# One converted weight block fewer ahead of the experts, four raw buffers, and product results in the ring of row tiles

## The chip, the cores and the metric

The kernel runs on one core of a Trainium2 chip, as a single program. Times are device microseconds (us) of one execution. Before the change three runs took 1015.66 us in the median (1014.09 to 1018.92).

## The reference

```python
# 1. a linear recurrence over time, for 4 batches x 8 heads, 768 steps, D = 48
a = a_re + i a_im, shortened to modulus <= 0.999
S_t = a_t * S_{t-1} + k_t v_t^T          # complex state, D x D
y_t = q_t @ Re(S_t)
x = y as 3072 rows of 384
# 2. one of 8 experts for each row, F = 1024
e = argmax(x @ w_gate);  p = softmax(x @ w_gate)[e]
x = p * (relu(x @ w1[e]) @ w2[e])
# 3. a gated layer; w1, w2, w3, w_out are doubles
out = ((x @ v1) * (x @ v2)) @ w3 @ w_out
```

The last two factors are one: the kernel makes `wf = w3 @ w_out` (1024 x 384) and multiplies by that.

## The kernel before, in words

The program has three stages on one time line. Up to about 407 us it works out the recurrence, in three groups of time steps with eight units each; the rows that come out (`xo`, tiles of 128 x 384 in a ring of six, `XB`) are routed in pairs: transposes `rt` (L122), logits `rl` (L131) copied to `lg` (L132), a chain on VectorE (`mx` L137, `key` L140, `kx` L142, `oh` L144), the rank of each row within its expert by a matmul `rk` (L148, L150), `r`, `pos`, `pi` on VectorE (L152 to L156), and an indirect DMA `xs<-xo,pi` on POOL that scatters the rows in DRAM by expert (L160). From about 444 us the experts run: `xe<-xs` (L385) reads one expert's rows, `px` (L395) transposes them, and 64 steps follow of nine matmuls into `ph` and nine into `py` each (L350 to L352, three for each product, since a weight or a value is a high and a low half). From about 700 us the last layer runs, with `wf` read back as `m2o`.

Beside that the kernel prepares `wf`. The class `Fuse` does it in two streams. The first converts doubles to a pair of fp32r halves in 24 conversion units: 8 factors `wo` of `w_out` (128 x 384), then 16 halves (128 x 512) of the 8 blocks of `w3`. Each unit has a raw buffer `fdr` of 512 KB, loaded from SyncE (SP) by `doubles` (L291), and three steps, of which the loop in `halves` runs the first for unit n beside the second for unit n-1 and the third for unit n-2: first VectorE's L336, L337, L339, then ScalarE's L329 and L330, then VectorE's L322, L323, L324. The raw buffer is free after L324. `ahead` issues the loads three units early. The second stream, `product`, makes the product blocks: 24 matmuls (L350 to L352) into `Wf`, or `wpo` within the experts, a ScalarE copy `ws` (L722), and a store `wf<-ws` by SP (L723). There is one buffer `ws`.

The constant `BEFORE` sets both how many blocks are converted by the end of the recurrence's third group, where `groups` (L1110 to L1145) runs one or two conversion units after each step of the recurrence's chain, and how many product blocks `build` issues ahead of the experts. `W3B` is the number of converted blocks kept at a time: `product` may run the next conversion units as long as `ready < min(f + W3B, BEFORE)`. The rest of the blocks, with their conversion units, are made within the experts, one piece for each step (`next(product, None)`). When the product stream has ended, its pools are left, and `moe2_weights` starts as the next stream in the experts: it loads `v1` and `v2` as `fdr<-in_v` from POOL (L291), converts them by `from_double` (L304 to L310), and reads `m2o<-wf` (L516), which `split` (L345, L346) turns into halves.

The order of each engine's instructions is set by the framework's scheduler, which simulates a time line and gives earlier-issued work the priority; `issue_after` moves a piece to the priority of another instruction. Pools and rings set the waits: a tile that takes a buffer waits until the last reader of its previous tile is done.

Of the kernel before, what the change touches and what calls it, by code (L numbers as in the profile page):

```python
# [8 lines left out]
F32 = mybir.dt.float32  # L9
F32R = mybir.dt.float32r  # L10
I32 = mybir.dt.int32
U32 = mybir.dt.uint32
U16 = mybir.dt.uint16
# [7 lines left out]
DM = 384  # L21
# [3 lines left out]
NF = 8  # L25
# [252 lines left out]
def ahead(load, srcs, n):  # L278

    got = []  # L280
    for i in range(len(srcs)):
        while len(got) < min(i + n, len(srcs)):
            got.append(load(srcs[len(got)]))
        yield got[i]


def doubles(pool, dma, bufs=RAW):

    def load(src):
        raw = pool.tile([128, 512, 2], I32, tag="fdr", name="fdr", bufs=bufs)[:, : src.shape[-1]]  # L290
        dma.dma_start(raw.rearrange("p n c -> p (n c)"), src.bitcast(I32))  # L291
        return raw

    return load
# [18 lines left out]
def halves(S, nc, raws, rest, units):  # L313

    v, act = nc.vector, nc.scalar
    first, second = [], []
    for n in range(len(units) + 2):
        if second:
            place, raw, m = second.pop()
            H, L = place()  # L320
            hi, lo = raw[:, :, 1].bitcast(F32), raw[:, :, 0].bitcast(F32)
            v.tensor_tensor(out=H, in0=hi, in1=m.bitcast(F32), op=ALU.mult)  # L322
            v.tensor_scalar(out=m, in0=H.bitcast(I32), scalar1=-0x800000, scalar2=None, op0=ALU.bitwise_and)  # L323
            v.scalar_tensor_tensor(out=L, in0=lo, scalar=2.0 ** -20, in1=m.bitcast(F32), op0=ALU.mult, op1=ALU.mult)  # L324
        if first:
            second.append(first.pop())
            _, raw, m = second[0]
            hi = raw[:, :, 1].bitcast(F32)
            act.activation(out=m, in_=m, func=AF.Relu, scale=8.0, bias=S.rebias)  # L329
            act.activation(out=hi, in_=hi, func=AF.Sign)  # L330
        if n < len(units):
            raw = next(raws)
            k = raw.shape[1]
            m = rest.tile([128, 512], I32, tag="fdm", name="fdm", bufs=2)[:, :k]
            low = rest.tile([128, 512], U16, tag="fdl", name="fdl")[:, :k]
            v.tensor_scalar(out=m, in0=raw[:, :, 1], scalar1=0x7FFFFE00, scalar2=None, op0=ALU.bitwise_and)  # L336
            v.tensor_scalar(out=low, in0=raw.bitcast(U16)[:, :, 2], scalar1=0x1FF, scalar2=None, op0=ALU.bitwise_and)  # L337
            lo = raw[:, :, 0]
            v.scalar_tensor_tensor(out=lo.bitcast(F32), in0=lo.bitcast(U32), scalar=2.0 ** -32, in1=low, op0=ALU.mult, op1=ALU.add)  # L339
            first.append((units[n], raw, m))  # L340
        yield
# [7 lines left out]
def mm3(nc, out, lh, ll, rh, rl, first, last):  # L349
    nc.tensor.matmul(out, lh, rh, start=first, stop=False)  # L350
    nc.tensor.matmul(out, lh, rl, start=False, stop=False)  # L351
    return nc.tensor.matmul(out, ll, rh, start=False, stop=last)  # L352
# [317 lines left out]
class Fuse:  # L670
# [10 lines left out]
    def _singles(self):  # L681
        nc, S, wp = self.nc, self.S, self.wp
        self.wo = [wp.tile([128, NF, DM], F32R, tag=f"wo{x}", name=f"wo{x}") for x in "hl"]
        self.w3 = []

        def factor(f):
            return lambda: [x[:, f] for x in self.wo]

        def block(f, h):
            def place():  # L690
                if not h:
                    pool = wp if f % W3B == 0 else self.w2p
                    self.w3.append([pool.tile([128, NF, 128], F32R, tag=f"w3{x}{f % W3B}", name=f"w3{x}{f}") for x in "hl"])
                return [x.rearrange("p g c -> p (g c)")[:, h * 512 : (h + 1) * 512] for x in self.w3[f]]
            return place

        srcs = [S.w_out[f * 128 : (f + 1) * 128, :] for f in range(NF)]
        srcs += [S.w3[f, :, h * 512 : (h + 1) * 512] for f in range(NF) for h in range(2)]
        raws = ahead(doubles(self.w2p, nc.sync, 5), srcs, 3)
        made = halves(S, nc, raws, wp, [factor(f) for f in range(NF)] + [block(f, h) for f in range(NF) for h in range(2)])  # L700
        for n in range(len(srcs) + 2):
            with self.tc.issue_after(S.end.ins):
                next(made)
            self.ready = max((n - 1 - NF) // 2, 0)
            yield

    def product(self):
        nc = self.nc
        for f in range(NF):
            while self.ready <= f:  # L710
                next(self.units)
                yield 0
            wh, wl = self.w3[f]
            po = self.psum(f, f"wpo_{f}")
            for g in range(NF):
                mm3(nc, po[:, :DM], wh[:, g], wl[:, g], self.wo[0][:, g], self.wo[1][:, g], g == 0, g == NF - 1)
                if g % 2 and g < NF - 1:
                    if self.ready < min(f + W3B, BEFORE):
                        next(self.units)
                    yield 960  # L720
            ws = self.w2p.tile([128, DM], F32, tag="ws", name=f"ws_{f}")
            nc.scalar.copy(ws, po[:, :DM])  # L722
            nc.sync.dma_start(self.S.wf[f * 128 : (f + 1) * 128, :], ws)  # L723
            self.blocks = f + 1
            yield 960
# [38 lines left out]
class Attn:  # L764
# [329 lines left out]
    def groups(self, route, side, free):  # L1094

        nc, S, st = self.nc, self.S, self.st
        self.ca, self.cb, self.cc, self.at, self.qkT, self.xs = {}, {}, {}, {}, {}, []
        self.route = route
        self.nv = self.slot = 0
        self.held = {}  # L1100
        self.pool, self.turns = [], 0
        self.spare = None
        self.vz = st.tile([128, VBUF, 2, HD], F32, tag="vz", name="vz")
        nc.gpsimd.memset(self.vz, 0.0)
        for q in range(2):
            self.ca[q] = st.tile([R2, 2, HD], F32, tag=f"ca{q}", name=f"ca{q}")
            self.cc[q] = st.tile([R2, 2, HD], F32, tag=f"cc{q}", name=f"cc{q}")
            nc.gpsimd.memset(self.ca[q], 0.0)
        yield lambda: self.made >= NPC
        self.W = self.pp.tile([128, 2, 512], F32, tag="W", name="W")  # L1110
        work = [(g, q, c) for g in range(NG) for q in range(2) for c in range(4)]
        ld = {}
        step = 0
        for n, u in enumerate(work):
            g, q, c = u
            if q == 0 and c == 0:
                while self.pool and self.made < (g + 1) * NPC:
                    yield self.fill(1)
                yield lambda: self.made >= (g + 1) * NPC
                yield from self.ends(g)  # L1120
                for x in work[n : n + 2]:
                    ld[x] = self.loads(x)
                if g == NG - 1:
                    yield free
                    singles = side.fuse.units
                    side()
            self.pool.append(Item("scores", self.scores(u, ld[u][1])))
            for x in self.chain(u, ld.pop(u)):
                yield x
                yield self.fill(S.fillcost)  # L1130
                step += 1
                if g == NG - 1:
                    for _ in range(1 + (step % 3 == 0)):
                        if side.fuse.ready < min(BEFORE, side.fuse.blocks + W3B):
                            next(singles, None)
            for x in work[n + 1 : n + 3]:
                if x[0] == g and x not in ld:
                    ld[x] = self.loads(x)
        self.spare = ()
        while self.pool:  # L1140
            yield self.fill(1)
# [138 lines left out]
FILL = 2600  # L1280
XB = 6
ZROWS = {i: [i] for i in range(NE)}
BEFORE = 6
W3B = 4


def build(ctx, tc, S):
# [8 lines left out]
    with ExitStack() as at:  # L1296
# [21 lines left out]
        def first():  # L1318
            z = x.ep.tile([128, 3 * DM // 8], F32, tag="zr", name="zr")
            nc.gpsimd.memset(z, 0.0)  # L1320
            yield from x.elementwise(lambda i: zero_rows(tc, S, z, ZROWS.get(i, [])), factors)
            for p in (e2, qp):
                p.__exit__(None, None, None)
            side.pools.append(tc.tile_pool(name="wf2", bufs=1, side="right"))
            side.fuse.w2p = side.pools[1].__enter__()
            done.append(1)
# [4 lines left out]
        drive([first(), second()])  # L1331
        while side.fuse.blocks < BEFORE:
            with tc.issue_after(x.lasty.ins):
# [62 lines left out]
```

## Time and profile before

| | us |
|---|---|
| median of three runs | 1015.66 (1014.09 to 1018.92) |
| the profiled execution | 1012.96 |
| its span, first to last instruction | 1011.2 |
| first matmul of the product (`Wf`) | 406.79 |
| first transpose of the experts (`px`) | 443.82 |
| first load `fdr<-in_v` issued | 501.23 |

The mean granted TensorE clock is 0.948 of full speed. The profile's first part gives the busy time and its share of the span for each engine: TensorE (PE) is busy for 896.7 us (89%), VectorE (DVE) for 610.1 us (60%), ScalarE (ACT) for 488.8 us (48%) and POOL for 126.8 us (13%). These are averages over three stages, so the rows further down are read by stretch. In all views a time is a start in us from the start of the span, and what stands in brackets is how long the engine stood idle before an instruction and what released it.

### The profile page before, as it was taken

Reading aid. Unit: us, or ns where it says so; the run is one execution under the profiler, and the core shown is the slowest. Engines: PE = TensorE matmul, PEld = TensorE weight load, DVE = VectorE, ACT = ScalarE, POOL = GpSimd, SP = SyncE. Lnnn points to the kernel's source line nnn. Section 1 sums busy time; section 2 is a strip of 40 time slices with the busy share of each in tenths; the row PEclk is TensorE's granted clock in tenths of the full one; section 3 lists DMA queues with packets and bytes.
Section 4 is the critical chain, followed back from the end, with each engine's and each line's share of the span. In section 5 each row is a group of like instructions: output and inputs, shape, how many; then the busy total and the mean of one; then the engine's idle time right before and its main releaser. Section 6 shows DMA issues by size and latency. Waiting matters only on the chain. (4 is left out here: it accounts for less than half of the span.)

```text
span 1011.2 us, 17058 instructions
## 1 busy us (share of the span) xinstructions
PE 896.7 (89%) x6402; PEld 762.8 (75%) x6402; DVE 610.1 (60%) x1374; ACT 488.8 (48%) x1089; POOL 126.8 (13%) x197
## 2 busy tenths in 40 slices
PE   3544899968897899969989999998999999999997
PEld 1222478655786787969978999997888888888886
DVE  6899899797996797545379996443232323232222
ACT  6455588764874786424355665453222222121211
POOL 5111000102010101000222221110001010101011
PEclk9666899989998999979999999999999999999999
DMA  5556985339544973544585765550000000000000
GB/s 188 178 177 197 293 264 180 127 110 346 167 162 132 345 241 104 164 124 131 127 267 163 190 155 131 141 92 2 1 1 32 1 32 1 32 1 32 2 30 31
DMA packets 90183, 128.74 MB, mean 127 GB/s; under 512 B 7233, under 2 KB 72689, under 8 KB 90097
## 3 DMA queue, kind: packets, MB, share of 16 engines
q1 hardware_dynamic: 76300, 82.61, 29.0%
q0 software_dynamic: 10688, 40.36, 11.3%
q10 hardware_dynamic: 3108, 4.65, 1.8%
q8 instruction: 51, 0.84, 0.3%
q14 instruction: 36, 0.29, 0.1%
HBM read 92.38 MB, written 35.22 MB: 126 GB/s over the span
## 5 line engine op out<-in xcount | busy, mean ns | idle before, releaser
L605 DVE TENSOR_TENSOR ab<-asb,pb 128x512 f32<-128x512 f32 x48 | 33.0, 688 | 188.2 <-PE pb L352 184.9
L346 DVE TENSOR_TENSOR l<-w,h 128x384 fp32r<-128x384 f32 x128 | 70.8, 556 | 70.4 <-ACT h L345 64.3
L345 ACT CAST h<-w 128x384 fp32r<-128x384 f32 x128 | 65.4, 514 | 98.2 <-PE ph L351 50.5
L600 ACT COPY asb<-pa 128x512 f32<-128x512 f32 x48 | 28.2, 586 | 121.1 <-PE pa L352 117.2
L804 PE MATMUL x<-s,ident 128*128 128x384 f32 x64 | 35.6, 692 | 48.6 <-ACT s L856 48.4
L345 ACT CAST gh<-ab 128x512 fp32r<-128x512 f32 x48 | 29.8, 620 | 95.2 <-DVE ab L605 90.7
L351 PE MATMUL py<-hl,h 128*128 128x432 f32 x192 | 70.4, 367 | 2.9 <-DVE hl L407 2.8
L350 PE MATMUL py<-hh,h 128*128 128x432 f32 x192 | 69.7, 363 | 2.8 <-ACT hh L406 2.8
L350 PE MATMUL ph<-xh,h 128*128 128x432 f32 x192 | 69.9, 366 | 0.2 <-DVE hl L407 0.2
L352 PE MATMUL ph<-xh,l 128*128 128x432 f32 x192 | 69.6, 363 | 0.0
L351 PE MATMUL ph<-xl,h 128*128 128x432 f32 x192 | 69.4, 361 | 0.0
L352 PE MATMUL py<-hh,l 128*128 128x432 f32 x192 | 69.3, 361 | 0.0
L848 DVE TENSOR_TENSOR pr<-cf,P 128x192 f32<-128x192 f32 x189 | 66.7, 354 | 3.1
L351 PE MATMUL po<-ol,gh 128*128 128x384 f32 x192 | 64.9, 338 | 0.0
L350 PE MATMUL po<-oh,gh 128*128 128x384 f32 x192 | 64.8, 337 | 0.0
L352 PE MATMUL po<-oh,gl 128*128 128x384 f32 x192 | 64.0, 338 | 0.0
L961 PE MATMUL tr<-ident,kk 128*96 128x128 f32 x384 | 57.1, 281 | 6.9 <-DMA kk<-qkd 3.9
L804 PEld LDWEIGHTS x<-s,ident 128*128 128x128 f32 x64 | 15.0, 257 | 63.6 <-ACT s L856 54.6
L569 POOL DMA_INDIRECT out<-ob,mdp x24 | 23.8, 993 | 305.9 <-DVE ob L568 164.2
L962 ACT COPY qkT<-tr 96x512 f32<-96x512 f32 x96 | 53.3, 589 | 16.2 <-PE tr L961 12.9
L350 PE MATMUL pa<-yh,ah 128*128 128x512 f32 x144 | 57.0, 396 | 3.0 <-ACT yh L345 3.0
L351 PE MATMUL pb<-yl,bh 128*128 128x512 f32 x144 | 57.0, 396 | 0.0
(219 smaller groups left out, 2388.2 us busy)
## 6 DMA issues: line engine op xcount, KB each, us to landing
w<-in_w SPq DMA_DIRECT2D x128, 192.0 KB
kk<-qkd SPq DMA_DIRECT2D x24, 768.0 KB
qkd<-qk POOLq DMA_DIRECT2D x21, 768.0 KB
qkr<-in_qk SPq DMA_DIRECT2D x24, 384.0 KB
a<-in_a SPq DMA_DIRECT2D x11, 768.0 KB
fdr<-in_w SPq DMA_DIRECT2D x16, 512.0 KB
fdr<-in_v POOLq DMA_DIRECT2D x12, 512.0 KB
xs<-zr POOLq DMA_DIRECT2D x8, 648.0 KB
```

The source lines that it names most:

```text
L345: nc.scalar.copy(H, src)
L346: nc.vector.tensor_tensor(out=L, in0=src, in1=H.bitcast(F32), op=ALU.subtract)
L350: nc.tensor.matmul(out, lh, rh, start=first, stop=False)
L351: nc.tensor.matmul(out, lh, rl, start=False, stop=False)
L352: return nc.tensor.matmul(out, ll, rh, start=False, stop=last)
L569: nc.gpsimd.indirect_dma_start(out=S.outv[j], out_offset=bass.IndirectOffsetOnAxis(ap=S.mdp[:, j, 0:1], axis=0), in_=ob, in_offset=None, b ...
L600: nc.scalar.copy(asb, pa)
L605: nc.vector.tensor_tensor(out=ab, in0=asb, in1=pb, op=ALU.mult)
L804: nc.tensor.matmul(p, S.ident, s[r], start=r == 0, stop=r == 1)
L848: v.tensor_tensor(out=pr, in0=twice(cf[i][:, t]), in1=bc(pv, 2, 1), op=ALU.mult)
L961: nc.tensor.transpose(pt[:, h], qk[:, h0 + h, w], self.S.ident)
L962: nc.scalar.copy(qkT[:, w, h0 : h0 + 4], pt)
```

## The change

`BEFORE` goes from 6 to 5 and `W3B` from 4 to 5. So 18 units are converted for the blocks ahead of the experts instead of 20, all five blocks fit into buffers of their own, and the third of the last three product blocks joins the two that the experts already held. The chain's steps issue one and two units in turn instead of two at each third step. There are four raw buffers (the default `RAW`) instead of five and loads are issued two units early instead of three. The converted blocks 0 and 1 of each five lie in the first pool, and the masks `fdm` in two single buffers of two pools instead of two buffers of one. `ws` takes a buffer of the ring `xo` of six.

```diff
--- before.py
+++ after.py
@@ -331,8 +331,8 @@
         if n < len(units):
             raw = next(raws)
             k = raw.shape[1]
-            m = rest.tile([128, 512], I32, tag="fdm", name="fdm", bufs=2)[:, :k]
-            low = rest.tile([128, 512], U16, tag="fdl", name="fdl")[:, :k]
+            m = rest[n % 2].tile([128, 512], I32, tag="fdm", name="fdm")[:, :k]
+            low = rest[0].tile([128, 512], U16, tag="fdl", name="fdl")[:, :k]
             v.tensor_scalar(out=m, in0=raw[:, :, 1], scalar1=0x7FFFFE00, scalar2=None, op0=ALU.bitwise_and)
             v.tensor_scalar(out=low, in0=raw.bitcast(U16)[:, :, 2], scalar1=0x1FF, scalar2=None, op0=ALU.bitwise_and)
             lo = raw[:, :, 0]
@@ -689,15 +689,15 @@
         def block(f, h):
             def place():
                 if not h:
-                    pool = wp if f % W3B == 0 else self.w2p
+                    pool = wp if f % W3B < 2 else self.w2p
                     self.w3.append([pool.tile([128, NF, 128], F32R, tag=f"w3{x}{f % W3B}", name=f"w3{x}{f}") for x in "hl"])
                 return [x.rearrange("p g c -> p (g c)")[:, h * 512 : (h + 1) * 512] for x in self.w3[f]]
             return place
 
         srcs = [S.w_out[f * 128 : (f + 1) * 128, :] for f in range(NF)]
         srcs += [S.w3[f, :, h * 512 : (h + 1) * 512] for f in range(NF) for h in range(2)]
-        raws = ahead(doubles(self.w2p, nc.sync, 5), srcs, 3)
-        made = halves(S, nc, raws, wp, [factor(f) for f in range(NF)] + [block(f, h) for f in range(NF) for h in range(2)])
+        raws = ahead(doubles(self.w2p, nc.sync), srcs, 2)
+        made = halves(S, nc, raws, (wp, self.w2p), [factor(f) for f in range(NF)] + [block(f, h) for f in range(NF) for h in range(2)])
         for n in range(len(srcs) + 2):
             with self.tc.issue_after(S.end.ins):
                 next(made)
@@ -718,7 +718,7 @@
                     if self.ready < min(f + W3B, BEFORE):
                         next(self.units)
                     yield 960
-            ws = self.w2p.tile([128, DM], F32, tag="ws", name=f"ws_{f}")
+            ws = self.S.rpool.tile([128, DM], F32, tag="xo", name=f"ws_{f}", bufs=self.S.xbufs)
             nc.scalar.copy(ws, po[:, :DM])
             nc.sync.dma_start(self.S.wf[f * 128 : (f + 1) * 128, :], ws)
             self.blocks = f + 1
@@ -1130,7 +1130,7 @@
                 yield self.fill(S.fillcost)
                 step += 1
                 if g == NG - 1:
-                    for _ in range(1 + (step % 3 == 0)):
+                    for _ in range(1 + step % 2):
                         if side.fuse.ready < min(BEFORE, side.fuse.blocks + W3B):
                             next(singles, None)
             for x in work[n + 1 : n + 3]:
@@ -1280,8 +1280,8 @@
 FILL = 2600
 XB = 6
 ZROWS = {i: [i] for i in range(NE)}
-BEFORE = 6
-W3B = 4
+BEFORE = 5
+W3B = 5
 
 
 def build(ctx, tc, S):
```

The scheduler then gives each engine another order. The first place is VectorE at the end of the recurrence, its last 12 instructions before the last step of the chain and the routing that follows it. `at` (L993) masks the scores, `cb` and `W` (L1061, L1062) are the chain's last step, and L322 to L324 and L336 to L339 are conversion steps. Before:

```order
L337 TENSOR_SCALAR fdl<-fdr 128x512
L137 TENSOR_REDUCE mx<-lg 128x2
L339 SCALAR_TENSOR_TENSOR fdr<-fdr,fdl 128x512
L140 SCALAR_TENSOR_TENSOR key_4620<-lg,mx,efirst 128x8 x2
L142 TENSOR_REDUCE kx_4623<-key_4620 128x2
L144 TENSOR_TENSOR oh_4625<-key_4620,kx_4623 128x16
L158 TENSOR_TENSOR run<-run,oh_4625 128x8 x2
L1061 TENSOR_TENSOR cb_4421<-W,T_3545 96x384
L993 TENSOR_TENSOR at_4704<-sc_4687,mask 128x512
L1062 TENSOR_TENSOR W<-W,T_3545 96x2x384
L152 TENSOR_TENSOR r_4656<-rk_4652,oh_4625 128x16
L154 TENSOR_REDUCE pos<-r_4656 128x2
```

After the change the last twelve are:

```order
L337 TENSOR_SCALAR fdl<-fdr 128x512
L324 SCALAR_TENSOR_TENSOR w3l_4494<-fdr,fdm 128x512
L339 SCALAR_TENSOR_TENSOR fdr<-fdr,fdl 128x512
L1061 TENSOR_TENSOR cb_4445<-W,T_3545 96x384
L336 TENSOR_SCALAR fdm<-fdr 128x512
L1062 TENSOR_TENSOR W<-W,T_3545 96x2x384
L337 TENSOR_SCALAR fdl<-fdr 128x512
L339 SCALAR_TENSOR_TENSOR fdr<-fdr,fdl 128x512
L137 TENSOR_REDUCE mx<-lg 128x2
L140 SCALAR_TENSOR_TENSOR key_4644<-lg,mx,efirst 128x8 x2
L142 TENSOR_REDUCE kx_4647<-key_4644 128x2
L144 TENSOR_TENSOR oh_4649<-key_4644,kx_4647 128x16
```

Before, one unit's first step (L337, L339) stands around `mx`, and no conversion stands behind it up to the end of the routing chain; after the change there are conversion steps ahead of `cb`, between `cb` and `W` and between `W` and `mx`, and the pair's routing (`mx` to `oh`) has come behind the chain's step.

The second place is PE behind the chain's last step, `W<-cb`. Before:

```order
L1008 MATMUL y_4594<-z_4339,qkT_4508 64x48
L1009 MATMUL y_4594<-vz,at_4592 64x48
L1046 MATMUL W<-cb_4421,perm 96x384 x2
L122 MATMUL rt_0_4745<-ident,xo_4643 128x128 x3
L1008 MATMUL y_4706<-z_4495,qkT_4645 64x48
L1009 MATMUL y_4706<-vz,at_4704 64x48
```

After the change:

```order
L147 MATMUL rk_4676<-run,ones 128x16
L131 MATMUL rl_1_4627<-wg,xt_1_4597 128x8 x3
L1046 MATMUL W<-cb_4445,perm 96x384 x2
L122 MATMUL rt_0_4769<-ident,xo_4667 128x128 x3
L148 MATMUL rk_4676<-oh_4649,upper 128x16
L150 MATMUL rk_4676<-oh_4649,ones 128x8
L1008 MATMUL y_4730<-z_4519,qkT_4669 64x48
L1009 MATMUL y_4730<-vz,at_4728 64x48
L1008 MATMUL y_4730<-z_4519,qkT_4669 64x48
```

Here `rk` is the rank matmul of a pair of rows. Before, `rk` of that pair stands some 25 rows ahead of `W<-cb`, among the matmuls of the unit before; after the change it stands between `W<-cb` and the last unit's `y` matmuls. Later, among the product's matmuls, the last pair's `rk` stands behind 109 of 144 before and behind 88 of 120 after.

The third place is ScalarE within the experts, around the copy of the last product block (`ws<-wpo`) and the first conversion of the second layer's weights (`m2raw<-fdr`, L305). `hh` is the ReLU of an expert's step, and `h` a half of an expert's weight. Before:

```order
L406 ACTIVATE hh<-ph 128x432
L722 COPY ws_5655<-wpo_5522 128x384
L345 CAST h_5673<-w_5531 128x384
L345 CAST h_5805<-w_5614 128x384
L406 ACTIVATE hh<-ph 128x432
L345 CAST h_5738<-w_5575 128x384
L305 ACTIVATE m2raw<-fdr 128x512
L345 CAST h_5853<-w_5665 128x384
L406 ACTIVATE hh<-ph 128x432
```

After the change:

```order
L406 ACTIVATE hh<-ph 128x432
L722 COPY ws_5917<-wpo_5765 128x384
L345 CAST h_6044<-w_5873 128x384
L345 CAST h_5928<-w_5774 128x384
L406 ACTIVATE hh<-ph 128x432
L305 ACTIVATE m2raw<-fdr 128x512
L345 CAST h_5993<-w_5822 128x384
L345 CAST h_6092<-w_5920 128x384
L406 ACTIVATE hh<-ph 128x432
```

In both lists L305 follows the `hh` after the last copy; the list of before has the block's copy about six expert steps earlier (its `h` are those of weights w_5477 to w_5665, after the change w_5820 to w_5993).

## Rows read from the trace of the kernel before

**Rows 1.** Windows by stage: time, then busy (instructions) of each engine, granted clock, DMA.
```profile
core 0: us, PE busy (x) PEld busy (x) DVE busy (x) ACT busy (x) POOL busy (x), PEclk, DMA share, GB/s
312.00:318.00 6.00, 5.54 (x25) 3.74 (x24) 3.17 (x8) 2.96 (x6) 0.00 (x0) 0.50 0.06 23
340.00:378.00 38.00, 36.73 (x563) 31.37 (x562) 38.00 (x95) 32.52 (x79) 2.24 (x2) 1.00 0.86 267
378.00:403.00 25.00, 24.28 (x389) 20.49 (x390) 20.08 (x55) 17.44 (x44) 2.44 (x2) 1.00 0.38 120
436.00:444.00 8.00, 0.18 (x1) 0.21 (x2) 1.71 (x4) 0.48 (x1) 0.00 (x0) 0.63 0.69 223
444.00:500.00 56.00, 56.00 (x294) 53.97 (x294) 24.77 (x56) 22.90 (x48) 2.14 (x2) 0.96 0.39 109
500.00:520.00 20.00, 17.28 (x90) 15.16 (x89) 13.80 (x28) 8.59 (x19) 6.21 (x10) 1.00 0.82 247
520.00:540.00 20.00, 16.81 (x75) 15.04 (x74) 14.90 (x31) 11.51 (x26) 8.06 (x9) 0.91 0.69 190
```
**Rows 2.** Timeline of PE, last chain step to the experts' first transpose.
```profile
402.28 1.50 PE L1046 MATMUL W<-cb,perm 96*96 96x384 f32 x4 [0.29 <-DVE r L152]
...
406.79 0.44 PE L350 MATMUL Wf<-woh,w3h 128*128 128x384 f32 x1
...
426.77 0.44 PE L350 MATMUL Wf<-woh,w3h 128*128 128x384 f32 x1 [1.20 <-ACT ws L722]
...
443.82 2.39 PE L395 MATMUL px<-ident,xe 108*128 108x108 f32 x12 [7.95 <-DMA xe<-xs]
```
**Rows 3.** Timeline of DVE, three instructions of conversion at full load.
```profile
370.75 0.42 DVE L323 TENSOR_SCALAR fdm<-w3h 128x512 int32<-128x512 int32 x1
371.08 0.69 DVE L339 SCALAR_TENSOR_TENSOR fdr<-fdr,fdl 128x512 f32<-128x512 uint32 x1
371.68 0.69 DVE L322 TENSOR_TENSOR w3h<-fdr,fdm 128x512 fp32r<-128x512 f32 x1
```
**Rows 4.** Timeline of DVE at the recurrence's end.
```profile
393.10 0.43 DVE L337 TENSOR_SCALAR fdl<-fdr 128x512 uint16<-128x512 uint16 x1 [0.98 <-DMA fdr<-in_w]
...
397.95 0.43 DVE L337 TENSOR_SCALAR fdl<-fdr 128x512 uint16<-128x512 uint16 x1 [1.44 <-DMA fdr<-in_w]
...
400.11 0.55 DVE L1061 TENSOR_TENSOR cb<-W,T 96x384 f32<-96x384 f32 x1
...
401.18 0.95 DVE L1062 TENSOR_TENSOR W<-W,T 96x768 f32<-96x768 f32 x1
```
**Rows 5.** Groups of DVE in 340:403, the raw wait: busy, mean ns, idle before.
```profile
L337 DVE TENSOR_SCALAR fdl<-fdr 128x512 uint16<-128x512 uint16 (+1 forms) x19 | 7.7, 407 | 3.6 <-DMA fdr<-in_w 3.6
```
**Rows 6.** Line L291 on SP in 388:396: issue ns, first and last start.
```profile
L291 SPq DMA_DIRECT2D fdr<-in_w x2: 328/328/328, 389.4 to 394.2; - x2
```
**Rows 7.** Window of the product, its own instructions: PE, PEld, ACT, clock, DMA.
```profile
407.00:436.00 29.00, 26.16 (x144) 24.65 (x143) 2.36 (x5) 1.00 0.54 166
```
**Rows 8.** Timelines of DVE, POOL and SP, the last pair's routing.
```profile
412.00 1.29 DVE L322 TENSOR_TENSOR w3h<-fdr,fdm 128x512 fp32r<-128x512 f32 x2 [9.38 <-PE Wf L351]
...
426.36 0.17 DVE L144 TENSOR_TENSOR oh<-key,kx 128x16 f32<-128x16 f32 x1
...
430.25 0.17 DVE L152 TENSOR_TENSOR r<-rk,oh 128x16 f32<-128x16 f32 x1
...
431.39 0.16 DVE L156 CAST pi<-pos 128x2 int32<-128x2 f32 x1
```
```profile
438.63 0.37 SPq L385 DMA_DIRECT2D xe<-xs  x1
```
**Rows 9.** Timelines of SP, POOL, DVE and ACT, second layer's weights.
```profile
496.60 0.44 SPq L723 DMA_DIRECT2D wf<-ws  x1
```
```profile
501.23 2.20 POOL L291 DMA_DIRECT2D fdr<-in_v  x4 [1.82 <-DMA wf<-ws]
```
```profile
507.11 0.43 DVE L304 TENSOR_SCALAR fda<-fdr 128x512 int32<-128x512 int32 x1 [5.01 <-DMA fdr<-in_v]
```
```profile
528.91 0.51 ACT L345 CAST oh<-m2o 128x384 fp32r<-128x384 f32 x1 [4.11 <-DMA m2o<-wf]
```

## The prediction

> **What bounds the kernel now.** I read the windows by stage first, then the timelines of the instructions between which time passes that PE doesn't use. The reader is to see three limits, one behind the other. In the recurrence's third group VectorE sets the pace: from 340 to 378 us it is busy for 38.00 of 38 us; from 378 to 403 us still for 20.08 of 25 [rows 1]. What it does beside the recurrence there is the conversion of doubles. Then PE has the product, from 406.79 us [rows 2]; the experts can't begin before the last pair of rows is ranked, scattered and read back, so `px` starts at 443.82 us, 37.0 us after the product's start, behind 7.95 us in which PE waits for `xe<-xs`. In the experts PE is the bound: 56.00 of 56 us busy from 444 to 500 us [rows 1]. Behind that, between 500 and 540 us, PE idles for 2.72 + 3.19 us (20 less 17.28, 20 less 16.81) [rows 1], where the second layer's weights come late [rows 9]. From there on the change touches nothing that I can find.
>
> So I add up four terms: the product's start, the way from it to `px`, the experts' PE work, and the stalls after 500 us.
>
> **1. The product's start: +5.5 us.** Before, the chain's steps convert until four blocks are ready (8 + 8 units), since `ready` is held below `blocks + W3B` = 4 while no product block exists; four more units follow beside the product, where VectorE sat idle for 9.38 us up to 412.00 us [rows 8]. After, five blocks are ready ahead of the product (18 units) and none follow until the experts. Two units of 128 x 512 thus move from a place where VectorE has room to one where it has little. A unit is three steps at the 0.33 us spacing of L323 (370.75 to 371.08) and three at the 0.60 us of the others (371.08 to 371.68) [rows 3]: 3 x 0.33 + 3 x 0.60 = 2.8 us, two are 5.6 us. Between 340 and 378 us nothing takes that up. Between 378 and 403 us VectorE idles for 25 - 20.08 = 4.9 us, but 3.6 us of all its idle from 340 to 403 us is the wait for raw loads [rows 5], of which 0.98 and 1.44 us stand at 393.10 and 397.95 us [rows 4]. Those waits stay, for the raw ring gets smaller: a load is issued when its buffer is free, and lands 3.7 us after its issue (389.4 to 393.10, 394.2 to 397.95) [rows 4, 6]. So 4.9 - 3.6 = 1.3 us of room is left: +4.3. With four buffers a unit's load can be issued only behind L324 of the unit four earlier; in the new order L337 of each unit always stands behind that L324. A load takes 3.7 us against 2.8 us for a unit, so each unit waits for 0 to 0.9 us, depending on how much of the recurrence's VectorE work lies between; for one wait more I take 0.8. And the last but one pair's `rk`, which stood ahead of `W<-cb`, now stands between it and the last `y`; its `oh` has the first step of another unit ahead of it, 0.4 us more than the chain's own. Sum +4.3 + 0.8 + 0.4 = +5.5. Bounds: if all of the 4.9 us of idle time takes the units in and the wait of 1.44 us goes with it, 5.6 - 4.9 - 1.4 = -0.7; if the raw waits of 3.6 us double, 5.6 + 3.6 = +9.2. I stay in the middle, nearer to the add-up by rows, since the order puts the units between `at`, `cb` and `W`, thus on the chain itself.
>
> The Trainium skill ("DMA: Bandwidth & Descriptors", section "Anatomy of one DMA — SWDGE (gpsimd) path") gives a transfer about 2.0 us and its bytes at 436 GB/s, so 512 KB would be an estimated 3.2 us; the rows show 3.7 us, here with loads from SP. By its figure the ring's wait would be 0.4 us for a unit at most and this term half a microsecond less; by the row it is as above, and the row decides.
>
> **2. From the product's start to `px`: -4.1 us.** The product ahead of the experts falls from 144 to 120 matmuls. The last pair's `rk` stood behind 109 of them and stands behind 88. At 26.16 us for 144, 0.18 us each [rows 7], these 21 are 3.8 us. The wait of 1.20 us for `ws` at 426.77 us [rows 2] lies ahead of that `rk` and goes with the ring of six, in which `ws` finds a buffer free. Against that VectorE's order has more conversion steps between `oh` and `r` and `r` and `pi` than before (two or three of 0.3 to 0.6 us): +0.9. From `pi` (431.39 us) to the issue of `xe<-xs` (438.63) are 7.2 us, and 5.2 us more to `px` [rows 2, 8]; these are transfers and stay. So -3.8 - 1.2 + 0.9 = -4.1 us. Bounds: -6 (nothing of the conversion in the way, and the pair's `oh` at 426.36 us early as well) to 0 (`oh` late, so that `rk` waits for VectorE, as the timeline shows 3.9 us between `oh` and `r`). PE will stand idle for longer ahead of `px`, some 9 to 10 us; that shifts no end.
>
> **3. The third block in the experts: +4.4 us.** 24 matmuls at 0.18 us [rows 7] in a stretch in which PE has no gap [rows 1]. At the experts' own pace, 56.00 us for 294, it is 4.6; should a gap take it in, 0. The two conversion units that move into the experts with it are 5.6 us of VectorE, which is busy for 24.77 of 56 us there: nothing.
>
> **4. The second layer's weights: -2.4 us.** POOL's load `fdr<-in_v` waited for the store `wf<-ws` of the last block (issued at 496.60, released at 501.23 us) since it reuses that pool's memory; VectorE's and ScalarE's first conversions stand in front of the experts' `hl` and `hh`, and wait for it until 507.11 us; PE lost 2.72 us by that [rows 1, 9]. After the change `ws` lies in the row tiles' ring, the loads wait only for the block's last matmuls and the raw units, and are issued some 4.6 us earlier relative to the last block's copy; in turn the product ends later, four expert steps ahead of the `hl` that stands behind the conversion instead of six. Four groups of nine matmuls are 36 x 0.19 = 6.9 us [rows 1]; load and first conversion take 507.11 - 501.23 = 5.9 us and the issue some 1 us, so 0.3 us of the 2.72 is left: -2.4. Bounds: -2.7 to +6 (rival 2). The stall behind `m2o<-wf`, 4.11 us on ScalarE and 3.19 on PE [rows 1, 9], stays, within 2 us either way.
>
> **Sum:** +5.5 - 4.1 + 4.4 - 2.4 = +3.4 us. Against the profiled execution's 1012.96 us this is 1016.4. That execution is 2.7 us below the median of the runs, 1015.66, so the time that I predict for the median is 1019.
>
> **Rivals.** *Slower by the ring and the clock.* Four buffers starve VectorE: each of the last six units or so waits for most of 0.9 us, +9 on the product's start, as the upper bound of term 1; PE then waits for `W` in more than one place between 395 and 412 us. Such gaps have a price of their own: in 444 to 500 us, behind the 7.95 us wait, the mean clock is 0.96, and in 312 to 318 us it is 0.50, at 5.54 us busy [rows 1, 2]. With 0.96 for 56 us, 56 x 0.04 / 0.5 = 4.5 us ran at the lower level (1.2 GHz), a loss of 2.2 us; the product would begin like that. +9 - 4.1 + 4.4 - 2.4 + 0 to 2.2 = +7 to +9: 1023 to 1025. It decides as soon as the waits for raw loads pass 6 us in the stretch. Against it: SP's loads have most of the DMA engines to themselves after 378 us (a share of 0.38).
> The Trainium skill says beside this ("TensorE: Matmul & The Clock Gate", section "Why this matters for your kernels") that idle gaps between bursts of matmuls put the clock back to its lower level; the rows at 312 and at 436 us agree, and no row shows yet that the gaps behind `W` are enough.
>
> *Slower by the load.* The pool's memory is still held by the last store, or by a later reader of it, so the load comes 4.6 us later than I think: term 4 turns from -2.4 to about +3.5 and the sum to +9: 1025.
>
> *Faster: the tail takes the units in.* The one and two units in turn spread the conversion more evenly, the 4.9 us of VectorE's idle time take in most of the two units, and the product starts -0.7 to +1.5 us from before. Then the sum is -3 to -0.6, and with -6 in term 2 down to -5: 1011 to 1015. For it: VectorE is idle for a fifth of the stretch; against it: most of that idle is a wait for the loads.
>
> **Chances.** My forecast 0.45, the ring 0.22, the load 0.08, the faster case 0.25. What a measurement can tell from no change is 0.5%, 5.1 us: under 1010.6 counts as faster, over 1020.7 as slower. The forecast's own range is 1015 to 1024, of which 0.16 of the 0.45 lies above 1020.7 (term 1's upper half) and 0.02 below 1010.6; the ring and the load are slower, 0.30 less 0.04 for their lower ends; of the faster case half, 0.13, passes 5.1 us, where terms 1 and 2 both stand at their better bounds or the stall of `m2o` shrinks too. That is 0.02 + 0.13 = 0.15 faster, 0.27 + 0.04 + 0.12 = 0.43 same and 0.16 + 0.26 = 0.42 slower. The range from 1010 to 1027 leaves out the ends of both sides.
>
> **What would show it.** The first `Wf` matmul at 411 to 413 us; L337's idle for raw loads from 340 us to the product's start over 3.6 us; `px` about 33 us behind the first `Wf` matmul; three `ws<-wpo` copies in the experts with PE without a gap; `fdr<-in_v` released by PE or a raw load and not by a store, and L304 with an idle time under 1 us. I am wrong if the product starts within 2 us of 406.8, if it starts over 9 us later, or if PE idles for more than 3 us ahead of the first second-layer conversion.

## The result and the profile after

The changed kernel takes 1023.17 us (median of 9 runs, 1020.36 to 1028.35), the kernel before 1014.04 us in the same comparison (9 runs): a ratio of 1.0096, 95% interval 1.007 to 1.0122. It is slower, by 7 to 12 us. The profiled execution has a span of 1021.6 us against 1011.2, and a mean granted clock of 0.927 against 0.948.

The windows of the changed kernel by stage, with the columns of [rows 1]:

```profile
374.00:378.00 4.00, 2.25 (x15) 1.65 (x15) 4.00 (x9) 3.28 (x9) 1.22 (x1) 0.95 0.79 216
378.00:390.00 12.00, 12.00 (x102) 9.87 (x102) 9.13 (x25) 4.88 (x10) 0.00 (x0) 0.50 0.31 94
...
390.00:410.00 20.00, 19.20 (x295) 16.04 (x294) 15.42 (x35) 14.63 (x38) 2.39 (x2) 0.97 0.44 130
410.00:419.00 9.00, 7.53 (x78) 5.99 (x78) 3.51 (x13) 2.57 (x6) 1.94 (x2) 0.62 0.19 72
...
452.00:510.00 58.00, 58.00 (x305) 55.91 (x306) 26.05 (x58) 23.60 (x49) 2.14 (x2) 0.96 0.40 108
...
530.00:550.00 20.00, 18.57 (x101) 17.18 (x100) 13.80 (x29) 9.89 (x22) 7.34 (x11) 1.00 0.81 239
550.00:570.00 20.00, 17.87 (x82) 16.38 (x81) 14.77 (x30) 10.59 (x24) 5.88 (x8) 0.91 0.74 213
```

The first two rows are what [rows 1] does not have: VectorE is as busy as before, but PE only for 2.25 of 4 us, and behind that TensorE's clock stands at its lower level, 0.50, for 12 us in which PE is never idle. From 410 to 419 us the mean is 0.62, so it stands there once more for some 7 of the 9 us. The same stretches of the kernel before:

```profile
372.00:376.00 4.00, 3.23 (x42) 2.73 (x37) 4.00 (x9) 2.86 (x10) 1.22 (x1) 1.00 0.68 212
376.00:388.00 12.00, 12.00 (x210) 10.57 (x210) 10.85 (x29) 9.96 (x24) 0.00 (x0) 1.00 0.46 140
```

In 12 us PE gets 210 instructions done there, 102 after the change. The timeline of PE after, at the pauses, at the product's start and at the first `px`:

```profile
374.84 0.55 PE L122 MATMUL rt<-ident,xo 128*128 128x128 f32 x3 [0.87 <-ACT xo L1012]
...
377.30 0.83 PE L961 MATMUL tr<-ident,kk 128*96 128x128 f32 x4 [0.91 <-ACT qkT L962]
...
418.73 0.44 PE L350 MATMUL Wf<-woh,w3h 128*128 128x384 f32 x1
...
451.85 1.50 PE L395 MATMUL px<-ident,xe 108*128 108x108 f32 x7 [9.67 <-DMA xe<-xs]
```

The product starts 11.9 us later than in [rows 2], `px` 8.0 us later. VectorE's groups from 334 to 418 us, with the columns of [rows 5]:

```profile
L337 DVE TENSOR_SCALAR fdl<-fdr 128x512 uint16<-128x512 uint16 (+1 forms) x22 | 8.9, 403 | 6.0 <-DMA fdr<-in_w 6.0
...
L152 DVE TENSOR_TENSOR r<-rk,oh 128x16 f32<-128x16 f32 x3 | 0.5, 172 | 3.4 <-PE rk L150 3.4
L137 DVE TENSOR_REDUCE mx<-lg 128x2 f32<-128x16 f32 x3 | 0.5, 162 | 2.6 <-ACT lg L132 2.6
```

The wait for raw loads grew from 3.6 to 6.0 us; another 6.0 us are waits of VectorE for PE and ScalarE, where there were 0.7 before. PE ran at half its speed in that stretch, and VectorE, on the path so far, waited for it.

The product's own window, and VectorE's steps of the last pair's routing, as in [rows 7, 8]:

```profile
419.00:442.00 23.00, 21.49 (x120) 20.48 (x119) 1.89 (x4) 1.00 0.53 165
```

```profile
423.97 1.30 DVE L322 TENSOR_TENSOR w3h<-fdr,fdm 128x512 fp32r<-128x512 f32 x2 [8.09 <-PE Wf L351]
...
433.90 0.17 DVE L144 TENSOR_TENSOR oh<-key,kx 128x16 f32<-128x16 f32 x1
...
437.71 0.16 DVE L152 TENSOR_TENSOR r<-rk,oh 128x16 f32<-128x16 f32 x1
...
438.92 0.17 DVE L156 CAST pi<-pos 128x2 int32<-128x2 f32 x1
```

`pi` stands 20.2 us behind the product's start (24.6 before), `px` 33.1 (37.0 before). And the second layer's weights, as in [rows 9]:

```profile
531.01 2.19 POOL L291 DMA_DIRECT2D fdr<-in_v  x4 [6.73 <-ACT ws L722]
```

```profile
538.12 0.43 DVE L304 TENSOR_SCALAR fda<-fdr 128x512 int32<-128x512 int32 x1 [3.20 <-DMA fdr<-in_v]
```

The load waits for `ws<-wpo` and no longer for a store; PE's stalls there are 1.43 and 2.13 us by the windows above (20 less 18.57 and 17.87), 2.72 and 3.19 before. From `px` to the end the span is 569.8 us (1021.6 - 451.85), 567.4 before.

So, net, the whole loss lies ahead of the product. From the tail's first `cb<-W` (L1061) to the first `Wf` matmul, which I call the tail below, it is 84.7 us (334.06 to 418.73) against 70.9 (335.87 to 406.79). The tail can be parted at VectorE's last chain step (L1062, at 401.18 us before and 409.80 after). Before, then after:

```profile
335.87:401.18 65.31, 62.82 (x956) 52.91 (x956) 60.54 (x154) 52.51 (x126) 4.68 (x4) 1.00 0.71 227
401.18:406.79 5.61, 4.77 (x98) 3.72 (x94) 1.36 (x5) 1.65 (x3) 1.94 (x2) 1.00 0.17 70
...
334.06:409.80 75.74, 70.69 (x987) 58.30 (x987) 64.57 (x154) 54.87 (x129) 4.87 (x4) 0.91 0.64 198
409.80:418.73 8.93, 7.46 (x79) 5.92 (x79) 3.71 (x14) 2.50 (x5) 1.77 (x2) 0.62 0.19 75
```

Up to that step VectorE is 4.0 us busier (64.57 less 60.54) and idles for 6.4 us more, 1.3 of it for loads and most of the other 5.1 for PE and ScalarE; behind it, at a mean clock of 0.62, come 3.3 us more.

### The profile page after: what moved, and what is told of

It reads as the page before. It is cut to its first block, busy times and chain, and to the rows that moved or that the text cites. A ratio compares the mean times of both kernels' runs of the same rounds, so it can differ in the third digit from the quotient of the medians.

```text
span 1021.6 us, 17063 instructions
## 1 busy us (share of the span) xinstructions
PE 912.8 (89%) x6402; PEld 775.4 (76%) x6402; DVE 611.9 (60%) x1374; ACT 489.0 (48%) x1089; POOL 126.7 (12%) x197
## 5 line engine op out<-in xcount | busy, mean ns | idle before, releaser
L351 PE MATMUL py<-hl,h 128*128 128x432 f32 x192 | 70.1, 365 | 2.4 <-DVE hl L407 2.4
L962 ACT COPY qkT<-tr 96x512 f32<-96x512 f32 x96 | 53.4, 587 | 14.2 <-PE tr L961 13.8
L350 PE MATMUL pb<-yh,bh 128*128 128x512 f32 x144 | 57.2, 398 | 0.0
```

Of the source, the lines that this page charges most:

```text
L962: nc.scalar.copy(qkT[:, w, h0 : h0 + 4], pt)
```

## The experiments

Each runs against the kernel before on its own chip. The scheduler's order up to the first raw load is the same in the kernel before, the changed one, e3, e6 and e10, while the profiled executions reach the tail's first `cb` at 334 to 343 us there; so I compare the length of the tail, and give the ratio of all runs beside it. One row stands for each: the tail as a window, with the columns of [rows 1]. For the kernel before and the changed kernel:

```profile
335.87:406.79 70.92, 67.59 (x1047) 56.63 (x1046) 61.91 (x157) 54.16 (x129) 6.62 (x6) 1.00 0.67 214
```

```profile
334.06:418.70 84.64, 78.12 (x1063) 64.22 (x1063) 68.28 (x167) 57.37 (x134) 6.61 (x6) 0.88 0.59 185
```

VectorE's 68.28 against 61.91 us are the two units: 6.4 us, where the prediction had 5.6. At a mean clock of 0.88, 2 x 0.12 x 84.6 = 20 us ran at the lower level.

**e1, only four blocks ahead of the product.**

```diff
-                        if side.fuse.ready < min(BEFORE, side.fuse.blocks + W3B):
+                        if side.fuse.ready < min(4, side.fuse.blocks + W3B):
```

> The changed kernel, but the chain's steps convert only until four blocks are ready (16 units), as before; four raw buffers, five product blocks ahead of the experts and ws in the row ring stay. Theory A (two more units on VectorE's full stretch are the first cause, the lower TensorE clock at 377 to 391 us follows from them): the first product matmul at 407 to 410 us instead of 418.7, no stretch at 0.50 clock between 370 and 400 us, and a time about 1012 to 1015 (the other terms sum to -2). Theory B (the ring of four raw buffers alone starves VectorE): product start still at 414 us or later, time 1019 or more. Theory C (the pace of one and two units): as B.

```profile
344.62:425.95 81.33, 74.55 (x1039) 62.00 (x1037) 67.65 (x164) 56.47 (x133) 5.16 (x4) 0.90 0.60 185
```

Ratio 1.0106 (1.0041 to 1.0172). The tail stays at 81.3 us, but A isn't tested by it: the groups of VectorE show ten halves of `w3` finished in this tail, as after the change, against eight in the kernel before (`product` issues the fifth block's units as well, and the scheduler put them into the tail).

```profile
L322 DVE TENSOR_TENSOR w3h<-fdr,fdm 128x512 fp32r<-128x512 f32 x10 | 6.9, 685 | 0.9 <-ACT fdr L330 0.8
```

**e2, the old pace.** `range(1 + (step % 3 == 0))` in place of `range(1 + step % 2)` in the changed kernel.

> The changed kernel with the old pace: two units at each third step of the chain instead of each second. Theory C (the pace puts units ahead of the chain's work at the wrong places): product start back by 4 us or more, to 414 us or earlier, and the 0.50 clock at 377 us gone. Theory A: the same number of units must be through before the product, so product start within 2 us of 418.7 and the time within 3 us of 1023. Theory B: the same as A.

```profile
335.68:419.00 83.32, 76.86 (x1049) 62.75 (x1046) 68.18 (x167) 56.36 (x133) 6.74 (x6) 0.89 0.60 186
```

Ratio 1.0121 (1.0027 to 1.0215), product start at 419.0 us. The tail is 1.3 us shorter, and the lower clock stays: the pace counts for little, and C fails.

**e3, four raw buffers alone; e5, the same with loads three units early; e6, five buffers with loads two units early.**

```diff
-        raws = ahead(doubles(self.w2p, nc.sync, 5), srcs, 3)
+        raws = ahead(doubles(self.w2p, nc.sync), srcs, 2)          # e3
+        raws = ahead(doubles(self.w2p, nc.sync), srcs, 3)          # e5
+        raws = ahead(doubles(self.w2p, nc.sync, 5), srcs, 2)       # e6
```

> The kernel before with four raw buffers and loads two units early, nothing else. Theory B: VectorE's waits for raw loads between 340 and 403 us rise from 3.6 us by 3 us or more, product start at 411 us or later, time slower by 4 us or more. Theory A: raw waits rise by 1 to 2 us, product start 407 to 409 us, time within 2 us of before.

> The kernel before with four raw buffers, loads still issued three units early. Theory D (the number of buffers: a load can't be issued before its buffer is free, however early it stands): as e3, the stretch from the tail's first cb to the product's first matmul at 76 to 80 us against 70.9, with 8 us or more at 0.50 clock. Theory E (the early issue alone): the stretch back to 71 to 73 us, clock 1.00.

> The kernel before with five raw buffers, loads issued two units early instead of three. Theory D: the fifth buffer lies idle when loads stand only two units early, so part of e3's loss shows: 72 to 76 us. Theory E: all of it, 77 to 79 us. If neither the number nor the early issue counts by itself: 71 us.

```profile
342.98:420.97 77.99, 73.12 (x1046) 59.81 (x1042) 62.42 (x152) 54.31 (x129) 4.92 (x4) 0.93 0.58 178
```

```profile
334.24:413.16 78.92, 73.80 (x1039) 60.71 (x1037) 62.33 (x152) 54.55 (x129) 4.88 (x4) 0.91 0.57 176
```

```profile
334.65:408.48 73.83, 70.71 (x1063) 59.45 (x1064) 61.91 (x157) 54.43 (x130) 6.61 (x6) 0.95 0.64 206
```

Ratios 1.0114 (1.008 to 1.0149), 1.0102 (1.0067 to 1.0137) and 1.0023 (0.9988 to 1.0057). Four buffers alone cost 1%, as much as the whole change; how early the loads stand in the code changes nothing: e5's order is e3's on every engine, and e6's is that of the kernel before. D holds, E falls. With four buffers the scheduler also writes another order: VectorE's in e3 leaves that of the kernel before at 351.7 us, 9 us into the tail. No run parts the buffer from this order. e6 is thereby a second look at the kernel before: its tail takes 73.8 us, with some 7 us at the lower clock, so the kernel before has such a fall in some executions too, and its tail differs by 3 us between the two. The number of raw waits alone doesn't give the loss: 6.0 us in e3 against 3.6 is 2.4 of 7.1 us.

**e7, e3 with PE's pause filled; e8, the changed kernel with the same.** 20 transposes are added to the logits of one pair of rows; their result is left unused.

```diff
             for j, xt in enumerate(xts):
+                if slot0 == 18 and i == 1:
+                    for _ in range(10):
+                        nc.tensor.transpose(pl[:, 128:256], S.ident, S.ident)
```

> e3 (four raw buffers, two units early) with 20 more transposes of 128 x 128 beside the logits of one pair of rows, which fill PE's pause ahead of the stretch at 0.50 clock; their result isn't used. Theory F (a pause of PE of 2 to 3 us brings the lower clock, and the lower clock makes most of the loss): clock 1.00 up to the product, the stretch at 72 to 75 us although PE does 2.3 us more. Theory G (the clock is a symptom; the late raw loads make the loss): the stretch at 78 us or more, whatever the clock.

> The changed kernel with the same 20 transposes in the same place. Theory F: the stretch from the first cb to the product falls from 84.6 to about 77 to 80 us (the two units more, and the lower clock behind the last chain step, stay), and the time by 4 to 7 us. Theory G: 84 to 87 us.

```profile
335.89:410.90 75.01, 70.38 (x1062) 58.97 (x1060) 61.97 (x152) 54.47 (x129) 5.06 (x4) 0.98 0.61 189
```

```profile
341.99:422.28 80.29, 72.74 (x1076) 60.65 (x1070) 67.92 (x164) 56.50 (x134) 6.34 (x4) 0.96 0.59 184
```

With more work for PE the tail gets shorter, by 3.0 us against e3 and 4.4 against the changed kernel, and e7's ratio falls to 1.0058 (1.0021 to 1.0095), which still overlaps that of e5 (1.0067 to 1.0137) on the same chip. The place of the pause, first in e3, then in e7:

```profile
382.00:388.00 6.00, 3.98 (x56) 3.23 (x54) 5.96 (x12) 4.88 (x15) 1.95 (x2) 1.00 0.55 157
388.00:398.00 10.00, 10.00 (x71) 7.96 (x69) 8.06 (x21) 4.18 (x8) 0.00 (x0) 0.50 0.38 107
```

```profile
374.30:380.30 6.00, 6.00 (x89) 5.54 (x87) 5.97 (x12) 4.48 (x14) 1.97 (x2) 1.00 0.54 157
380.30:390.30 10.00, 9.15 (x129) 7.58 (x125) 9.24 (x24) 7.54 (x20) 0.00 (x0) 1.00 0.49 156
```

PE busy for 3.98 of 6 us: the clock falls, and 10 us bring 71 instructions. PE busy for 6.00 of 6: the clock stays, and 10 us bring 129. G falls. F holds as to the clock, but that the lower clock makes most of the loss isn't shown: of the 7 to 8 us that four buffers add to the tail (e3, e5) the filling gives back 3 to 4, at a mean clock of 0.98, and some of VectorE's steps stand in another order in e7 as well. e8's ratio, 1.0109 (1.0063 to 1.0155), shows no gain beside that of the changed kernel. The 4.4 us of its tail are lost again behind it:

```profile
459.01 2.39 PE L398 MATMUL px<-ident,xe 108*128 108x108 f32 x12 [12.52 <-DMA xe<-xs]
```

`px` comes 36.7 us behind the product's start, not 33.1, and from the tail's first `cb` to `px` it is 117.0 us against 117.8 in the changed kernel. That the lower clock costs the changed kernel's whole run anything is thus read from its rows, and not shown by taking the pause away.

**e4, five product blocks and `ws` in the row ring, with five raw buffers and four converted blocks kept.**

```diff
-BEFORE = 6
+BEFORE = 5
-            ws = self.w2p.tile([128, DM], F32, tag="ws", name=f"ws_{f}")
+            ws = self.S.rpool.tile([128, DM], F32, tag="xo", name=f"ws_{f}", bufs=self.S.xbufs)
```

> The kernel before (five raw buffers, four converted blocks kept, old pace) with five product blocks ahead of the experts and ws in the row ring alone. By terms 2 to 4 of the prediction: product start as before (406.8 us within 1.5), 33 us from there to the first px, third block +4.4 and second-layer load -2.4, thus about -2 us against before. Theory B and C: the same. If the prediction's terms 2 to 4 are wrong, px is not 3 to 5 us nearer to the product's start.

```profile
337.87:408.80 70.93, 68.20 (x1063) 57.15 (x1061) 61.99 (x157) 54.43 (x130) 6.67 (x6) 1.00 0.66 214
```

```profile
428.27 0.17 DVE L144 TENSOR_TENSOR oh<-key,kx 128x16 f32<-128x16 f32 x1
...
432.16 0.17 DVE L152 TENSOR_TENSOR r<-rk,oh 128x16 f32<-128x16 f32 x1
...
433.30 0.16 DVE L156 CAST pi<-pos 128x2 int32<-128x2 f32 x1
```

```profile
445.62 2.39 PE L395 MATMUL px<-ident,xe 108*128 108x108 f32 x12 [13.39 <-DMA xe<-xs]
```

Ratio 1.0007 (0.9969 to 1.0045). The tail is that of the kernel before. But `px` comes 36.8 us behind the product's start, not 33: with 24 matmuls fewer, the last pair's `oh` and `pi` stand 19.5 and 24.5 us behind it, as before (19.6 and 24.6). PE just waits longer, 13.39 us. The last pair hangs on VectorE's conversion steps. From the product's start to that `oh` VectorE has, before and after the change:

```profile
406.79:426.36 19.57, 18.79 (x115) 18.43 (x113) 10.95 (x27) 8.57 (x19) 0.00 (x0) 1.00 0.59 182
```

```profile
418.73:433.90 15.17, 15.17 (x96) 15.14 (x94) 7.79 (x20) 7.56 (x17) 0.18 (x1) 1.00 0.67 204
```

21 conversion steps stand ahead of it before and in e4, 15 in the changed kernel and in e2 (`px` 34.1 us behind the product's start). That two units have left is not enough for it: e1 and e8 finish ten halves ahead of the product too, and have 21 steps there and `px` at 36.8 and 36.7 us. It is the order that the scheduler wrote.

```profile
462.78 2.39 PE L395 MATMUL px<-ident,xe 108*128 108x108 f32 x12 [12.89 <-DMA xe<-xs]
```

**e9, two units more with five raw buffers.** The first two units of `w_out` are converted twice.

```diff
-        srcs = [S.w_out[f * 128 : (f + 1) * 128, :] for f in range(NF)]
+        units = [*range(NF), 0, 1]
+        srcs = [S.w_out[f * 128 : (f + 1) * 128, :] for f in units]
...
-            self.ready = max((n - 1 - NF) // 2, 0)
+            self.ready = max((n - 1 - len(units)) // 2, 0)
```

> The kernel before with five raw buffers, where the first two units (128 x 384 of w_out) are converted twice: 18 units stand ahead of the product as in the change, by 2 x 2.2 us of VectorE's time, with the raw ring as before. The prediction's count for the moved units (room of 1.3 us, the rest on the path): first cb to product 70.9 + 3 = 73 to 75 us, clock 1.00. Theory F (VectorE later, PE pauses, clock lower): 77 us or more with 8 us or more at 0.50. If the tail takes them in: 71 to 72 us.

```profile
336.57:414.67 78.10, 72.31 (x1063) 58.77 (x1063) 66.41 (x169) 56.46 (x134) 6.72 (x6) 0.96 0.63 203
```

```profile
336.57:406.45 69.88, 66.08 (x995) 54.47 (x995) 65.44 (x168) 55.66 (x133) 4.78 (x4) 1.00 0.69 222
406.45:414.67 8.22, 6.23 (x68) 4.29 (x68) 0.96 (x1) 0.80 (x1) 1.95 (x2) 0.58 0.12 48
```

```profile
407.56 2.84 PE L1047 MATMUL W<-cb,perm 96*96 96x384 f32 x4 [2.42 <-DVE W L1063]
```

Ratio 1.0101 (1.0053 to 1.0149): two units alone cost 1% too, so the costs of the units and of the ring do not add up in the changed kernel. 4.5 us more of VectorE (66.41 less 61.91) cost 7.2 us of tail. Up to VectorE's last chain step these are 4.6 us, at a clock of 1.00, near the prediction's count (2 to 4). There PE waits for VectorE for 2.42 us, and the way from there to the product takes 8.22 us instead of 5.61, at a mean clock of 0.58. The tail lies between the two forecasts.

**e10, `ws` in the row ring alone; e11, with six raw buffers, loads four units early; e12, as e11 with `BEFORE = 5`.**

```diff
-            ws = self.w2p.tile([128, DM], F32, tag="ws", name=f"ws_{f}")
+            ws = self.S.rpool.tile([128, DM], F32, tag="xo", name=f"ws_{f}", bufs=self.S.xbufs)
-        raws = ahead(doubles(self.w2p, nc.sync, 5), srcs, 3)
+        raws = ahead(doubles(self.w2p, nc.sync, 6), srcs, 4)       # e11 and e12 only
```

> The kernel before with ws in the ring of row tiles, nothing else. By terms 2 and 4 of the prediction: the wait of 1.20 us for ws goes, product start to px 36 us against 37.0; the second layer's load no longer waits for a store, PE's stall there falls from 2.72 us to under 1; together -2 to -4 us. If the second layer's load is held by something else: -1 to 0.

> As e10, with six raw buffers and loads four units early. If raw loads hold up VectorE in the kernel before too (3.57 us from the first cb to the product), the waits fall to 1 us or less and the stretch to 68 to 70 us: -3 to -6 us in all. If the stretch of the kernel before is set by VectorE's work and PE alone: as e10, stretch 70.5 to 71.

> As e11, with five product blocks ahead of the experts. e4 showed product start to px at 36.8 us with five blocks, so the block moved into the experts is not paid back: 2 to 4 us slower than e11. If the sixth raw buffer lets the last pair's routing come earlier beside the product, px at 33 to 35 us from its start and the time within 1 us of e11.

```profile
339.83:413.75 73.92, 70.44 (x1064) 59.53 (x1064) 61.94 (x157) 54.53 (x130) 10.52 (x6) 0.95 0.65 206
```

```profile
340.86:420.06 79.20, 75.32 (x1061) 62.69 (x1057) 63.18 (x159) 54.92 (x130) 8.78 (x6) 0.91 0.61 198
```

```profile
336.99:414.79 77.80, 71.27 (x1063) 59.49 (x1063) 63.17 (x159) 55.16 (x131) 8.59 (x6) 0.98 0.63 203
```

e10 takes 1015.13 us against 1018.93, a ratio of 0.996 (0.9932 to 0.9989): faster than the kernel before, and so the best of all here. What it gains stands behind `px`:

```profile
508.12 0.43 DVE L304 TENSOR_SCALAR fda<-fdr 128x512 int32<-128x512 int32 x1 [2.56 <-DMA fdr<-in_v]
```

VectorE waits for the second layer's load for 2.56 us instead of 5.01, and PE idles for 0.89 us from 507 to 527 us, where it was 2.72 in the kernel before [rows 1]; the wait for `ws` itself was worth nothing, `px` comes 37.3 us behind the product's start. A sixth raw buffer does not help: 1.002 (0.9992 to 1.0048), and e12 1.0056 (1.0035 to 1.0078). The scheduler writes another order for it from the first conversions on, with a tail of 79.2 us at a clock of 0.91. Which of its rows makes the pause is open.

## Why the prediction was right, and where it was not

The direction held, and the time came out 4 us above the forecast (1023.17 against 1019), inside its range of 1010 to 1027. There is luck in that: the sum of +3.4 us was less than the 5.1 us that the prediction itself counts as no change, and the medians are 9.1 us apart. By steps:

- **Term 1 was mis-sized: +5.5 forecast, +11.9 measured.** That is over the 9 us which the prediction named as its sign of being wrong. Its parts for VectorE were near: up to the last chain step 4.0 us more of work and 1.3 us more of waits for loads, 5.3 together, and 4.6 for two units in e9. What the sum left out was the price of the lower clock, which stood in the rival only, and with 0 to 2.2 us. It is the 5.1 us of VectorE's other waits and most of the 3.3 us behind the last chain step, an estimate of about 8 us.
- **How sure the clock's share is.** Two more estimates frame it. In e6, with the order and VectorE's work of the kernel before (61.91 us both), some 7 us at the lower clock made the tail 2.9 us longer; at that price 20 us cost 8. If half of the time at the lower level is taken off each tail, the tails with five raw buffers and 16 units are 70.1 to 70.9 us (the kernel before, e4, e6, e10), those with four buffers and 16 units 71.8 and 72.5 (e5, e3), and those with 18 units 73.2 to 75.0 (e1, e2 74.2, the changed kernel 74.5, e9); that would be 10 us of clock, an upper bound, since from 409.80 us on PE is not busy throughout (7.46 of 8.93 us) and since e8 (77.1) and e12 (76.2) do not fit. So its size is argued from rows; no run takes the lower clock away alone.
- **The first rival came nearest, at too low a chance (0.22).** It said 1023 to 1025, and raw waits came to 6.0 us, just the point named. But its sum put 9 us on the raw waits and at most 2.2 on the clock; measured are 2.4 us more of raw waits and about 8 us of clock, so that its time fits is in part luck. Nor do the rows show that raw waits bring PE's pauses: at 374.84 and 377.30 us PE waits for ScalarE's copies, while VectorE is busy for 4.00 of 4 us, and in e9 the clock falls with the raw ring as it was.
- **Term 2 was right in size, -4.1 forecast and -3.9 measured, and wrong in its reason: luck.** Not the 21 matmuls fewer ahead of `rk` count (e4), but six conversion steps fewer ahead of `oh` in the order that the scheduler happened to write (e1 and e8 do not have it). The prediction also had no conversion beside the product after the change, and two units in the experts. The trace has six halves of `w3` between the product's start and `px`, eight before, and none behind `px` in either kernel; `w3h` goes on there at 423.97 us, as it did at 412.00 us [rows 8].
- **Terms 3 and 4, +4.4 - 2.4 = +2.0 forecast, +2.4 measured from `px` to the end.** PE has no gap from 452 to 510 us; the two stalls shrink by 2.4 us in all, 1.3 of it in the first, where I had all of it. L304 waits for 3.20 us, not under 1, since POOL's load was released by the copy `ws`, and not by the last matmuls.
- The other rivals fell: the load was not held by a store, and the tail did not take the units in.

## What to carry to other kernels

Where two engines share a stretch and both are near full, a little more work or waiting on the one can cost more than its length: here 5.3 us more on VectorE went with a tail 13.8 us longer, and in the rows PE's pauses, a granted clock of 0.50 and VectorE's waits for PE follow each other. Read the granted clock in windows of a few us, and put a price on the fall in the forecast itself, not in a rival. A change made of several edits is best taken apart first: here one of them (`ws` in the row ring) gains 0.4% alone, and another (one raw buffer fewer, to pay for a converted block) loses 1% alone, with the order that comes with it. Fewer instructions ahead of a step only help if that step waits for this engine: with 24 matmuls fewer, `pi` in e4 stood where it was.

## What the runs showed of the hardware

The clock fell behind pauses of PE of 0.87 and 0.91 us with work between them (2.25 of 4 us busy), with no single wait over 0.91 us there; it stayed at 1.00 in the kernel before, where PE was busy for 3.23 of 4 us in the same place. The Trainium skill ("TensorE: Matmul & The Clock Gate", section "Why this matters for your kernels") warns of idle gaps between bursts; these rows show a fall behind two short ones. It then stood at 0.50 for 12 us while PE was busy throughout. And one program, its order the same on every engine (the kernel before and e6), showed a tail at 1.00 in one profile and one with some 7 us at the lower level in another.
